# Strassen's scheme for the feed-forward's first product of the last two blocks of tokens

## The chip, the core and the metric

The kernel runs on one core of a Trainium2 chip. The metric is the device time of one execution in microseconds (us): 754.23 is the median of three executions before the change. An execution that is profiled also leaves a trace, and the engines are named as there: PE is the matrix engine (its weight loads are a row of their own, PEld), DVE the vector engine, ACT the scalar engine, POOL the general one, SP the queue that issues the DMAs.

## The reference

Causal attention with a decay, then a feed-forward (MoE) layer, then a second one with a softmax in it:

```
scores = q k^T / sqrt(64) + decay, causal;  x = softmax(scores) v            # 4 batches, 8 heads, 576 positions
h  = x @ w_in                                                                # 2304 x 512 @ 512 x 2048
y  = maximum(0.01*h, h) @ w_out                                              # 2304 x 2048 @ 2048 x 512
h2 = y @ w2_in                                                               # 2304 x 512 @ 512 x 1024
s  = h2 * softmax(h2);  ln = (s - mean(s)) / sqrt(var(s) + 1e-6) * g_ln
out = ln @ w2_out                                                            # 2304 x 1024 @ 1024 x 512
```

All of it is fp32. The kernel keeps that precision by splitting each operand into a high and a low fp16 part, so that one product takes three matmuls (high x high, high x low, low x high).

## The kernel before, in words

**Stages.** The 2304 tokens are nine blocks of 256. Attention fills the blocks (block 6 and 7 last, tiles `x`). The feed-forward goes through them in `ORDER` = 0, 1, 4, 5, 3, 2, 8, 6, 7, each in two halves g of the hidden dimension (18 units `ffn(blk, g)`). A unit has four pieces k: `hidden` (L988) computes 256 hidden columns of a block in one PSUM tile `ps_f` with 24 matmuls of 256 columns, ACT and DVE turn it into the fp16 pair `g`; then 96 matmuls multiply the four `g` by `w_out` (L1036) into `ps_f`, and the result goes to DRAM (`yp_d`). The second layer (`load_y`, `layer2`, `normal`, `layer2_out`) loads a block's y again, makes the sums that Strassen's scheme wants, and computes its first product with seven products in place of eight (`layer2`, L1083): each is six matmuls of 512 columns. Two of the seven go to `p1` and two to `p2`; each of these is one PSUM tile `ph` of 1024 columns, which is two banks, and a product fills one half of it (`bank`, L1089). DVE joins them (`plus` L1103, `full` L1106), `normal` makes softmax and layer norm, a transposing DMA turns the result, and `layer2_out` multiplies by `w2_out` (24 matmuls of 512 columns for 128 tokens).

**Weights.** `whole` (L898) joins a loaded weight chunk, `split` makes the fp16 pair. `split_w2i` (L959) makes the mixed weights of `layer2`. All weights lie in tiles `wz` of 2 KB a partition: 27, eight more when attention's `qa` is done, and 14 (`NWY`, named `wy`) when attention's memory is opened by `phase2` (L1217).

**The order.** A planner written out in the kernel (`Plan.run`, L195) orders everything. Every operation has a priority (smaller goes first), costs from formulas (L378 to L402) and the buffers it reads and writes, which can be a part of a tile: `(Z, 0)` is one part of Z, and parts don't wait for each other in the plan. Whenever a modelled engine is free, the planner takes the ready operation with the smallest priority and emits it at once. So the program's order, over all engines, is the order of the modelled starts. Each engine then works through its own instructions in that order, and semaphores, which the framework below sets from the order in which instructions touch a tile, hold them apart. Unit n of the feed-forward has priority 1000 + 21.76 n, `layer2` of the t-th block `L2P[t]` (1300 and up), its outputs `OUTP[t]`, the second layer's weights 930 to 950, attention 100 to 470.

Of the kernel before, what the change touches and what calls it, by code (L numbers as in the profile page):

```python
# [7 lines left out]
F32 = mybir.dt.float32  # L8
# [16 lines left out]
NG = NC // 2  # L25
# [16 lines left out]
AV = -2.05  # L42
EP = 1307.15
LD = 10.04
# [14 lines left out]
NYO = 2  # L59
NWY = 14  # L60
NY2 = 2
NHL2 = 2
NTR = 3
PWL = 500.0
DMAR = 320.0
YB_ENGS = ("DVE",)
VB_ENGS = ("DVE",)
# [9 lines left out]
US0 = 21.76  # L77
HST = 2.56
TB = 256
# [43 lines left out]
WEIGHT = {"DVE": 7.06}  # L123
WEIGHT2 = {"DVE": 1.06}
HEAT = 0.25
# [252 lines left out]
def dve(n):  # L378
    return 1.042 * n + 70
# [26 lines left out]
def body(tc, kqa, kq, vt, f, wa, w2i, w2o, gln, out):  # L406
# [491 lines left out]
    def whole(src, prio, lead=None):  # L898

        s, k, low = staged(src, prio, lead)  # L900
        z = P.buf("wz")
        P.op(DVE, dve(512), lambda: joined(z.t.bitcast(I32), low, k), prio, w=[z], r=[s, k], lock=True)
        return z
# [117 lines left out]

    def ffn(blk, g, prio):
        eprio = prio - EP
        first, last = blk not in YO, LEFT.setdefault(blk, 2) == 1
        LEFT[blk] -= 1
# [3 lines left out]
        if first:  # L1029
            YO[blk], YPD[blk] = [P.buf("yo") for q in range(2)], []  # L1030
        gs = {k: hidden(k, XB[blk], prio + HST * i, eprio + i) for i, k in enumerate(GRP[g])}
        for q in range(2):
            ps, yo = P.buf("ps_f"), YO[blk][q]
            for d in range(2):

                def pe(d=d, q=q, ps=ps):  # L1036
                    for k in GRP[g]:
                        for i in range(2):
                            y_mms(ps.t[:, TB * d:TB * d + TB], 2 * k + i, 2 * q + d, gs[k], k == GRP[g][0] and i == 0, k == GRP[g][-1] and i == 1)

                P.op(PE, 6 * len(GRP[g]) * mmr(TB), pe, prio + YD + 4 * q + 2 * d, r=list(gs.values()) + [WO[2 * k + i] for k in GRP[g] for i in range(2)],
                     **({"w": [ps]} if d == 0 else {"rw": [ps]}))
# [14 lines left out]
    def load_y(blk, prio):  # L1057
        yw, sy, y = P.buf("yw"), P.buf("sy"), P.buf("y2")
        for q in range(2):
# [14 lines left out]
        sub_f(X(2), A(1, 0), X(1), 256, prio, S_ENGS, w=[(sy, 2)], r=[yw, (sy, 1)])  # L1074
        pieces = [(512 * e, 512, lambda e=e: four(yw.t[:, 0:1024])[:, e::2], (yw, "e%d" % e)) for e in range(2)] + [(1024, 768, lambda: four(sy.t), sy)]
        for at, n, v, k in pieces:
            copy_f(lambda at=at, n=n: four(y.t[:, 0, at:at + n]), v, n, prio, scale=lambda: ev(IY + blk), w=[(y, (0, at))], r=[k, (EX, ("iy", blk))])
        for at, n, v, k in pieces:
            sub_f(lambda at=at, n=n: four(y.t[:, 1, at:at + n]), v, lambda at=at, n=n: four(y.t[:, 0, at:at + n]), n, prio, scale=lambda: ev(IY + blk),
                  w=[(y, (1, at))], rw=[k], r=[(y, (0, at)), (EX, ("iy", blk))])  # L1080
        return y

    def layer2(tb, y, prio, oprios):  # L1083
# [7 lines left out]
        def prod(p, at, n, pr):  # L1091

            def pe():
                for k in range(2):
                    yh, yl = (y.t[:, j, at + 128 * k:at + 128 * k + 128] for j in range(2))
# [5 lines left out]
            P.op(PE, 6 * mmr(512), pe, pr, r=[y, W2I[0, n], W2I[1, n]], w=[p])  # L1101

# [26 lines left out]
    def normal(tt, blk, ps, st, eprio, oprio):  # L1129
# [57 lines left out]
    with tc.manual_schedule():  # L1187
# [44 lines left out]
        P.op(CTL, 1.0, phase2, 0.0, deps=attn_ops)  # L1232
        P.weight = WEIGHT2
# [63 lines left out]
```

## Time and profile before

| | |
|---|---|
| time, median of 3 executions | 754.23 us (752.92 to 755.57) |
| the profiled execution's own time | 756.95 us |
| its span in the trace | 755.2 us, 15580 instructions |
| busy PE, DVE, ACT, POOL | 698.0, 535.7, 502.6, 324.3 us |
| granted clock of PE, mean | 0.997 |

The span runs from the first to the last instruction; the own time has 1.75 us around it. Busy shares are means over stages with different limits, so the stretches count, not the totals. Matmuls are pipelined: a row's duration holds the time in the pipe, and the price of one matmul is the distance between starts.

### The profile page before, as it was taken

The page shows a single profiled execution, that of the slowest core. Times are in us where ns is not written, and L with a number is a line of the kernel's source. Part 1 is how long each engine was busy: PE and PEld are TensorE (multiplying, and loading weights), DVE is VectorE, ACT ScalarE, POOL GpSimd, SP SyncE. Part 2 cuts the span into 40 slices and gives each one's busy share as a digit, 9 for nine tenths or more (in the row PEclk, how much of TensorE's full clock was granted, in tenths as well). Part 3 has the DMA queues.
Part 4 walks back from the last instruction along what each step waited for, and adds up shares of the span by engine and source line. Part 5 has one row for each costly group of instructions (what it writes and reads, how often), then busy time and mean ns, then how long its engine had stood idle before and what let it go on. Part 6 is the DMA issues. An engine that isn't in the chain of part 4 may idle for free.

```text
span 755.2 us, 15580 instructions
## 1 busy us (share of the span) xinstructions
PE 698.0 (92%) x5603; PEld 533.8 (71%) x5603; DVE 535.7 (71%) x1420; ACT 502.6 (67%) x1160; POOL 324.3 (43%) x439
## 2 busy tenths in 40 slices
PE   0558789999999999999999999999999999999997
PEld 0346678788788888888889888688866665444443
DVE  5988789878878887777875964351657558788760
ACT  2698999897878789999895666312635435444551
POOL 4466878894365158646522481000422213132220
PEclk9999999999999999999999999999999999999999
DMA  7989489747548766667875414010023242343343
GB/s 214 312 240 230 110 215 232 129 102 158 140 96 164 143 160 128 132 136 148 180 125 142 144 40 154 1 57 1 30 57 84 70 84 81 87 112 70 85 93 102
DMA packets 163902, 94.18 MB, mean 125 GB/s; under 512 B 144224, under 2 KB 144240, under 8 KB 163824
## 3 DMA queue, kind: packets, MB, share of 16 engines
q1 hardware_dynamic: 163792, 93.17, 52.2%
q8 instruction: 44, 0.72, 0.4%
q14 instruction: 34, 0.28, 0.1%
q10 hardware_dynamic: 32, 0.02, 0.0%
HBM read 47.95 MB, written 10.06 MB: 77 GB/s over the span
## 4 chain that ended last, share of the span: by engine, by line
PE 70%; ACT 9%; DVE 5%; DMA 3%; issue 2%; POOL 1%; SPq 0%; ACTq 0%; POOLq 0%; DVEq 0%
PE ps_f L524 47%; PE ps_g L524 8%; PE ps_s L524 6%; PE ph L524 5%; PE ps_v L524 4%; DMA wst<-wa 2%; ACT ps_s L734 2%; ACT hl L478 1%; DVE hl L489 1%; ACT xr L818 1%; ACT kq L478 1%; DVE VT L489 1%; ACT ps_f L1003 1%; DMA pt<-hl 1%; ACT wz L478 1%
## 5 line engine op out<-in xcount | busy, mean ns | idle before, releaser
L524 PEld LDWEIGHTS <-wz 128*128 128x128 f16 x2700 | 262.5, 99 | 39.5 <-issue 5.5
L524 PE MATMUL ps_f<-g,wz 128*128 128x256 f16 x828 | 104.8, 276 | 0.2 <-DVE g L1004 0.2
L489 DVE SCALAR_TENSOR_TENSOR hl<-ps_s,st,hl 128x512 f16<-128x512 f32 (+4 forms) x160 | 82.0, 538 | 17.6 <-ACT hl L478 16.2
L734 ACT ACTIVATE ps_s<-ps_s,st 128x512 f32<-128x512 f32 (+4 forms) x160 | 78.7, 492 | 9.9 <-DVE st L787 8.7
L524 PE MATMUL ps_f<-dec,wz 128*128 128x256 f16 x684 | 84.5, 273 | 0.0
L478 ACT ACTIVATE hl<-ps_s,st 128x512 f16<-128x512 f32 (+4 forms) x157 | 76.6, 524 | 8.9 <-DVE st L755 3.5
L493 POOL TENSOR_TENSOR kq<-raw,kq 64x576 fp32r<-64x576 f32 x64 | 78.2, 1225 | 8.5 <-ACT kq L478 4.1
L524 PEld LDWEIGHTS <-qa 128*128 128x128 f16 x756 | 72.8, 98 | 10.3 <-issue 2.0
L524 PEld LDWEIGHTS <-tr 128*128 128x128 f16 x432 | 42.2, 98 | 49.9
L524 PE MATMUL ps_v<-pt,VT 128*128 128x128 f16 (+1 forms) x928 | 60.3, 216 | 13.2 <-DVE xr L821 9.1
L524 PEld LDWEIGHTS <-y 128*128 128x128 f16 x378 | 36.6, 98 | 45.6 <-issue 3.7
L787 DVE CUSTOM_DVE_ANT_0 ps_s<-ps_s,mask 128x128 f32<-128x128 f32 (+3 forms) x128 | 62.3, 494 | 7.6 <-PE ps_s L524 6.2
L524 PEld LDWEIGHTS <-VT 128*128 128x128 f16 x928 | 53.1, 101 | 20.3 <-issue 9.2
L524 PE MATMUL ps_f<-x,wz 128*128 128x256 f16 x528 | 66.1, 279 | 0.0
L524 PE MATMUL ps_s<-kq 128*128 128x512 f32 (+5 forms) x256 | 60.8, 366 | 1.6 <-DVE hl L489 1.5
L1004 DVE TENSOR_TENSOR g<-ps_f,g 128x512 f16<-128x512 f32 x40 | 27.5, 686 | 26.3 <-ACT ps_f L1003 25.6
L524 PEld LDWEIGHTS ps_s<-kq 128*128 128x128 f32 (+1 forms) x256 | 40.9, 191 | 7.0 <-issue 1.3
L524 PE MATMUL ps_f<-sd,wz 128*128 128x256 f16 x330 | 45.0, 273 | 0.0
L821 DVE SCALAR_TENSOR_TENSOR xr<-ps_v,xr 64x256 f32<-64x256 f32 (+1 forms) x96 | 33.9, 353 | 15.3 <-ACT xr L818 13.9
L1003 ACT ACTIVATE ps_f<-ps_f 128x512 f32<-128x512 f32 x72 | 42.5, 590 | 0.3
L524 PE MATMUL ps_f<-wst,wz 128*128 128x256 f16 x330 | 42.3, 273 | 0.0
L1004 DVE TENSOR_TENSOR dec<-ps_f,dec 128x512 f16<-128x512 f32 x32 | 22.0, 687 | 26.7 <-ACT ps_f L1003 26.5
(252 smaller groups left out, 1382.3 us busy)
## 6 DMA issues: line engine op xcount, KB each, us to landing
wst<-wa SPq DMA_DIRECT2D x32, 512.0 KB
raw<-kq SPq DMA_DIRECT2D x16, 480.0 KB
VT<-vt SPq DMA_DIRECT2D x16, 320.0 KB
raw<-yp_d SPq DMA_DIRECT2D x18, 256.0 KB
raw<-w2i SPq DMA_DIRECT2D x8, 512.0 KB
raw<-w2o SPq DMA_DIRECT2D x8, 512.0 KB
out<-ot SPq DMA_DIRECT2D x16, 256.0 KB
raw<-kqa SPq DMA_DIRECT2D x12, 256.0 KB
```

Of the source, the lines that this page charges most:

```text
L478: nc.scalar.activation(o, i, CP, scale=1.0 if scale is None else scale)
L489: nc.vector.scalar_tensor_tensor(o, a, scale, b, op0=ALU.mult, op1=ALU.subtract)
L493: (nc.vector if eng == DVE else nc.gpsimd).tensor_tensor(o, a, b, op=op)
L524: nc.tensor.matmul(o, lhsT=l, rhs=r, start=start, stop=stop)
L734: P.op(ACT, act(W, 1, True) + 93, lambda view=view, j=j, k=k: nc.scalar.activation(view(), view(), AF.Exp, bias=sts.t[:, j:j + 1], scale=- ...
L787: P.op(DVE, dve(W) + 130, lambda i=i, j=j, view=view: nc.vector.tensor_tensor_reduce(view(), view(), mask[:, 512 - 128 * i:640], -0.125, 3 ...
L818: P.op(ACT, act(n, 1, True), lambda: nc.scalar.activation(xr.t[a:a + 64, dst0:dst0 + n], ps.t[b:b + 64, c0:c1], CP, scale=PS), prio, w=[(x ...
L821: P.op(DVE, dve(n) + 60, lambda: nc.vector.scalar_tensor_tensor(xr.t[a:a + 64, dst0:dst0 + n], ps.t[a:a + 64, c0:c1], PS, xr.t[a:a + 64, d ...
L1003: P.op(ACT, act(512, 0, True), lambda: nc.scalar.activation(ps.t, ps.t, AF.Prelu, scale=GS, alpha=0.01), eprio, rw=[ps])
L1004: P.op(DVE, dve(512) + 60, lambda: nc.vector.tensor_tensor(g.t[:, 1], ps.t, g.t[:, 0], op=ALU.subtract), eprio, w=[(g, 1)], r=[ps, (g, 0)])
```

## The change

The last two blocks, 6 and 7, go through the feed-forward's first product together, first for g = 1, then for g = 0 (`PU`). For each of the eight pieces k, `hidden2` takes the place of two calls of `hidden`: seven products of six matmuls (256 columns) instead of 48 matmuls. The first two products, P1 and P6, lie in the halves of one `ps_f` tile X, P5 in half of another, Y, and the four results C11, C12, C21, C22 in the quarters of one `ph` tile Z (C11 and C12 in its first bank). ACT copies P1, and seven sums on DVE make the results. `mixed_w` makes the mixed weights of a piece from the fp16 pairs (into a tile `wt`), `mixed_x` the mixed tokens of the two blocks (into four `wz`). Both work from the moment when attention's memory is open. The second layer's weights are joined only after the last of this mixing (`deps=mixed[-1:]`). `wy` has 3 tiles for 14; eight `wt` tiles are new, and as they come free they become `y2a`, `tr` and `hl2`, which the second layer had as tiles of its own. The second product of block 7 gets its own priorities (`PYS`). The softmax of the second layer waits for its own block's scale (`("s", blk)`) and no longer for the scale of `w2_out` (`"u2"`).

```
-EP = 1307.15
+EP = 1514.57
-NWY = 14
-NY2 = 2
-NHL2 = 2
-NTR = 3
+NWY = 3
+T_HEIRS = ("y2a", "tr", "tr", "hl2", "tr", "tr", "hl2")
-YB_ENGS = ("DVE",)
+YB_ENGS = ("DVE", "ACT")
-HST = 2.56
+HST = 2.72
-GS = 2.0 ** -24
+GS = 2.0 ** -20
+PU = (((6, 7), 1), ((6, 7), 0))
+PYS = (17.44, 130.99)
+WTP = (955.0, 965.0)
+XSP = 959.06
+MX = 3
-L2P = (1300.0, 1366.2, 1370.0, 1390.0, 1410.0, 1430.0, 1450.0, 1470.0, 1476.09)
-OUTP = (1340.0, 1370.0, 1398.97, 1420.38, 1440.0, 1496.99, 1472.1, 1500.0, 1520.0)
-LYP = -1744.46
+L2P = (1300.0, 1366.2, 1370.0, 1388.69, 1410.0, 1428.49, 1437.78, 1470.0, 1476.09)
+OUTP = (1340.0, 1370.0, 1398.97, 1420.38, 1440.0, 1496.99, 1472.1, 1514.45, 1520.0)
+LYP = -4034.93
-WEIGHT2 = {"DVE": 1.06}
+WEIGHT2 = {"DVE": 2.51}
+M_ENGS = ("DVE", "POOL")
+MH_ENGS = ("ACT", "DVE", "POOL")
...
     def load_w2i(k, h, prio):
-        z = ZI[j] = whole(w2i[k, h], prio)
+        z = ZI[j] = whole(w2i[k, h], prio, None, mixed[-1:])
     def load_w2o(c, prio):
-        z = ZQ[c] = whole(w2o[c], prio)
+        z = ZQ[c] = whole(w2o[c], prio, None, mixed[-1:])
...
+    def mixed_w(k, prio, after):
+        za, zb, n, t = P.buf("wz"), P.buf("wz"), P.buf("wz"), P.buf("wt")
+        half = lambda z, h: lambda: z.t[:, 256 * h:256 * h + 256]
+        for z, c in ((za, 2 * k), (zb, 2 * k + 1)):
+            sub_f(lambda z=z: z.t, lambda c=c: W(WI[c], 0), lambda c=c: W(WI[c], 1), 512, prio, M_ENGS, op=ALU.add, w=[z], r=[WI[c]], deps=after)
+        sub_f(half(n, 0), half(zb, 1), half(zb, 0), 256, prio, M_ENGS, w=[(n, 0)], r=[zb])
+        sub_f(half(za, 0), half(zb, 0), half(za, 0), 256, prio, M_ENGS, rw=[(za, 0)], r=[zb])
+        sub_f(half(n, 1), half(zb, 1), half(za, 0), 256, prio, M_ENGS, w=[(n, 1)], r=[zb, (za, 0)])
+        sub_f(half(za, 1), half(za, 1), half(n, 1), 256, prio, M_ENGS, rw=[(za, 1)], r=[(n, 1)])
+        for i, z in enumerate((n, za)):
+            d = lambda j, i=i: pair_of(t.t)[:, j, 512 * i:512 * i + 512]
+            copy_f(lambda d=d: d(0), lambda z=z: z.t, 512, prio, engs=MH_ENGS, w=[(t, (0, i))], r=[z])
+            sub_f(lambda d=d: d(1), lambda z=z: z.t, lambda d=d: d(0), 512, prio, M_ENGS, w=[(t, (1, i))], r=[z, (t, (0, i))])
+        WT[k] = t
+    def mixed_x(p, prio, after):
...
+    def hidden2(k, p, prio, eprio):
+        X, Y, Z, u, ga, gb = P.buf("ps_f"), P.buf("ps_f"), P.buf("ph"), P.buf("hr"), P.buf("g"), P.buf("g")
...
+        P1, P6, P5, C11, C12, C21, C22, r1, u2, u3 = (X, 0), (X, 1), (Y, 0), (Z, 0), (Z, 1), (Z, 2), (Z, 3), (u, 0), (u, 1), (u, 2)
+        for i, (o, xt, xb, w, wb) in enumerate((
+                (P1, old(a11), a11, wold(wa_, 0), wa_), (P6, new(x2), x2, wnew(256), t), (C11, old(a12), a12, wold(wa_, 256), wa_),
+                (C22, new(x3), x3, wnew(0), t), (P5, new(x1), x1, wnew(512), t), (C12, new(x4), x4, wold(wb_, 256), wb_), (C21, old(a22), a22, wnew(768), t))):
...
+            P.op(PE, 6 * mmr(TB), pe, prio + 0.2 * i, w=[o] + ([(ga, "slot"), (gb, "slot")] if i == 0 else []), r=[xb, wb])
+        P.op(ACT, act(256, 0, True), lambda: nc.scalar.activation(at(r1)(), at(P1)(), CP), eprio, w=[r1], r=[P1])
+        def plus(o, a, b, **kw):
+            P.op(DVE, dve(256) + 60, lambda: nc.vector.tensor_tensor(at(o)(), at(a)(), at(b)(), op=ALU.add), eprio, **kw)
+        plus(u2, P6, r1, w=[u2], r=[P6, r1])
+        plus(C11, C11, r1, rw=[C11], r=[r1])
+        plus(u3, C22, u2, w=[u3], r=[C22, u2])
+        plus(C22, P5, u3, rw=[C22], r=[P5, u3])
+        plus(u2, P5, u2, rw=[u2], r=[P5])
+        plus(C12, C12, u2, rw=[C12], r=[u2])
+        plus(C21, C21, u3, rw=[C21], r=[u3])
+        for e, g in enumerate((ga, gb)):
...   # as in hidden: two activations on ACT, one subtraction on DVE, for each of the two blocks
-    def ffn(blk, g, prio):
+    def ffn(blks, g, prio):
...
+            both = {k: hidden2(k, blks, prio + 2 * HST * i, eprio + i) for i, k in enumerate(GRP[g])}
+            gs = [{k: x[e] for k, x in both.items()} for e in range(2)]
+        for blk, gk, at in zip(blks, gs, (YD,) if len(blks) == 1 else PYS):
+            ffn_out(blk, g, gk, prio + at, eprio)
...
-            E(), ps.t, AF.Exp, ..., w=[Eb, (st, 1)], r=[ps, (st, 0), (EX, "u2")])
+            E(), ps.t, AF.Exp, ..., w=[Eb, (st, 1)], r=[ps, (st, 0), (EX, ("s", blk))])
...
+            P.tag("wt", tiles(bp, "wt", NG, [128, 1024], F32))
+            P.tag("g", tiles(bp, "g", 4, [128, 2, 512], F16))
+            P.tag("hr", tiles(bp, "hr", 2, [128, 768], F32))
...
+        for blks, g in [((x,), g) for x, g in UN] + [((x,), g) for x in ORDER for g in range(2) if (x, g) not in UN and (x, g) not in paired] + list(PU):
+            ffn(blks, g, 1000.0 + US0 * n)
+            n += len(blks)
```

`mixed_x` has twelve additions or subtractions of 512 columns and four copies, in the manner of `mixed_w`.

## Rows read from the trace of the kernel before

**Rows 1.** Busy time by stretch: us, then PE, PEld, DVE, ACT, POOL (x instructions), clock, DMA.
```profile
412.00:440.00 28.00, 28.00 (x260) 25.16 (x258) 23.64 (x50) 19.77 (x37) 14.63 (x15) 1.00 0.33 115
440.00:479.00 39.00, 39.00 (x359) 34.89 (x357) 18.40 (x31) 20.46 (x44) 13.92 (x14) 1.00 0.23 82
479.00:520.00 41.00, 40.79 (x334) 32.49 (x333) 16.78 (x41) 8.81 (x16) 1.42 (x2) 1.00 0.07 26
520.00:560.00 40.00, 40.00 (x340) 32.99 (x338) 23.94 (x43) 21.54 (x37) 14.40 (x18) 1.00 0.18 41
640.00:700.00 60.00, 59.70 (x279) 27.12 (x277) 48.47 (x115) 28.50 (x41) 14.14 (x27) 1.00 0.38 92
```
**Rows 2.** Chain that ended last, in order of time: start us, us, what.
```profile
442.26 36.70 PE ps_f L524 x336
746.20 5.19 PE ps_g L524 x24
```
**Rows 3.** What PE waited for, 440 to 756: us in total, times, longest.
```profile
PE ph L524 <- DVE sd L1104: 1.4, 2, 1.2
```
**Rows 4.** Timeline of PE, end of a block's seven products: start us, us, engine, operation.
```profile
485.92 0.81 PE L524 MATMUL ph<-sd,y 128*128 128x512 f16 x3
486.94 0.81 PE L524 MATMUL ph<-wst,y 128*128 128x512 f16 x3 [0.21 <-DVE sd L1104]
...
648.34 0.81 PE L524 MATMUL ph<-sd,y 128*128 128x512 f16 x3
649.30 0.81 PE L524 MATMUL ph<-wst,y 128*128 128x512 f16 x3
...
689.36 0.81 PE L524 MATMUL ph<-wz,y 128*128 128x512 f16 x3
...
702.31 0.81 PE L524 MATMUL ph<-sd,y 128*128 128x512 f16 x3
704.29 0.81 PE L524 MATMUL ph<-wst,y 128*128 128x512 f16 x3 [1.17 <-DVE sd L1104]
```
**Rows 5.** Timeline of DVE beside it.
```profile
648.50 0.69 DVE L1108 CUSTOM_DVE_ANT_0 ph<-ph,wst 128x512 f32<-128x512 f32 x1
649.11 0.14 DVE L1108 DVE_READ_ACCUMULATOR2_ANT s<- 128x1 f32 x1
...
690.21 0.70 DVE L1108 CUSTOM_DVE_ANT_0 ph<-ph,wst 128x512 f32<-128x512 f32 x1 [1.54 <-PE ph L524]
...
703.55 0.68 DVE L1104 TENSOR_TENSOR sd<-ph,sd 128x512 f32<-128x512 f32 x1
704.15 2.35 DVE L493 TENSOR_TENSOR hl<-raw,hl 128x1024 f16<-128x1024 f32 x2
```
**Rows 6.** Prices by form, 440 to 755: line engine op tile shapes xcount | busy us, mean ns | idle.
```profile
L1002 ACT ACTIVATE g<-ps_f 128x512 f16<-128x512 f32 x12 | 7.1, 594 | 18.0 <-PE ps_f L524 18.0
L1104 DVE TENSOR_TENSOR sd<-ps_g,wst 128x512 f32<-128x512 f32 x6 | 4.1, 685 | 1.4 <-PE ps_g L524 1.4
L493 DVE TENSOR_TENSOR raw<-raw 128x256 f32<-128x256 f32 x6 | 2.9, 492 | 0.0
L493 DVE TENSOR_TENSOR wy<-x,wy 128x512 f32<-128x512 f32 x1 | 0.7, 678 | 0.0
L489 DVE SCALAR_TENSOR_TENSOR wz<-wy,ex,wz 128x512 f16<-128x512 f32 x3 | 2.2, 744 | 0.6 <-POOL wz L485 0.6
```
**Rows 7.** Operations on tile xr, 380 to 440: ns min/median/max, first and last start us, forms.
```profile
L818 ACT ACTIVATE xr<-ps_v x9: 216/376/382, 382.7 to 410.6; 64x256 f32<-64x256 f32 x5, 64x64 f32<-64x64 f32 x4
L821 DVE SCALAR_TENSOR_TENSOR xr<-ps_v,xr x9: 205/405/428, 383.6 to 411.0; 64x256 f32<-64x256 f32 x5, 64x64 f32<-64x64 f32 x4
L493 POOL TENSOR_TENSOR x<-xr,x x3: 669/671/1029, 384.6 to 411.9; 128x256 f16<-128x256 f32 x3
```
**Rows 8.** Lines L896 and L1178 from 380 on, same columns; then PE's timeline.
```profile
L896 DVE SCALAR_TENSOR_TENSOR sd<-raw,wk x2: 671/682/693, 400.5 to 529.8; 128x512 int32<-128x512 int32 x2
L1178 ACT ACTIVATE ot<-ps_g,ex x8: 668/687/688, 565.7 to 751.5; 128x512 f32<-128x512 f32 x8
...
490.85 0.82 PE L524 MATMUL ps_f<-sd,wz 128*128 128x256 f16 x6
...
635.96 1.46 PE L524 MATMUL ps_f<-wz,tr 128*128 128x512 f16 x6
```

More of the change, by code (lines that the diff above doesn't have):

```diff
@@ L896, in joined, with whole @@
         nc.vector.scalar_tensor_tensor(o, low(), 13, k.t, op0=ALU.logical_shift_right, op1=ALU.bitwise_or)
-    def whole(src, prio, lead=None):
+    def whole(src, prio, lead=None, deps=()):
         s, k, low = staged(src, prio, lead)
         z = P.buf("wz")
-        P.op(DVE, dve(512), lambda: joined(z.t.bitcast(I32), low, k), prio, w=[z], r=[s, k], lock=True)
+        P.op(DVE, dve(512), lambda: joined(z.t.bitcast(I32), low, k), prio, w=[z], r=[s, k], deps=deps, lock=True)
         return z
@@ L1020, in body @@
     YO, LEFT = {}, {}
-    def ffn(blk, g, prio):
-        eprio = prio - EP
+    WT, SX, mixed = {}, {}, []
+    pair_of = lambda t: t.bitcast(F16).rearrange("p (j n) -> p j n", j=2)
+    def mixed_w(k, prio, after):
[12 more added lines that the diff above has]
+        WT[k] = t
@@ new lines, in mixed_x @@
+    def mixed_x(p, prio, after):
+        (a11, a12), (a21, a22) = XB[p[0]], XB[p[1]]
+        z11, z12, z21, n = (P.buf("wz") for _ in range(4))
+        x = lambda a, j: lambda: a.t[:, j]
+        v = lambda z: lambda: z.t
+        for z, a in ((z11, a11), (z21, a21), (z12, a12)):
+            sub_f(v(z), x(a, 0), x(a, 1), 512, prio, M_ENGS, op=ALU.add, w=[z], r=[a], deps=after)
+        sub_f(v(n), v(z11), v(z21), 512, prio, M_ENGS, w=[n], r=[z11, z21])
+        for j in range(2):
+            sub_f(v(z21), v(z21), x(a22, j), 512, prio, M_ENGS, op=ALU.add, rw=[z21], r=[a22])
+        sub_f(v(z11), v(z21), v(z11), 512, prio, M_ENGS, rw=[z11], r=[z21])
+        sub_f(v(z12), v(z12), v(z11), 512, prio, M_ENGS, rw=[z12], r=[z11])
+        out = []
+        for z in (z21, z11, n, z12):
+            t = P.buf("wz")
+            copy_f(lambda t=t: as_g(t.t)[:, 0], v(z), 512, prio, engs=MH_ENGS, w=[(t, 0)], r=[z])
+            sub_f(lambda t=t: as_g(t.t)[:, 1], v(z), lambda t=t: as_g(t.t)[:, 0], 512, prio, M_ENGS, w=[(t, 1)], r=[z, (t, 0)])
+            out.append(t)
+        SX[p] = out
@@ new lines, in ffn @@
+    def ffn(blks, g, prio):
+        eprio = prio - EP
+        if len(blks) == 1:
+            gs = [{k: hidden(k, XB[blks[0]], prio + HST * i, eprio + i) for i, k in enumerate(GRP[g])}]
+        else:
+            both = {k: hidden2(k, blks, prio + 2 * HST * i, eprio + i) for i, k in enumerate(GRP[g])}
+            gs = [{k: x[e] for k, x in both.items()} for e in range(2)]
+        for blk, gk, at in zip(blks, gs, (YD,) if len(blks) == 1 else PYS):
+            ffn_out(blk, g, gk, prio + at, eprio)
@@ L1039, in pe @@
                             y_mms(ps.t[:, TB * d:TB * d + TB], 2 * k + i, 2 * q + d, gs[k], k == GRP[g][0] and i == 0, k == GRP[g][-1] and i == 1)
-                P.op(PE, 6 * len(GRP[g]) * mmr(TB), pe, prio + YD + 4 * q + 2 * d, r=list(gs.values()) + [WO[2 * k + i] for k in GRP[g] for i in range(2)],
+                P.op(PE, 6 * len(GRP[g]) * mmr(TB), pe, prio + 4 * q + 2 * d, r=list(gs.values()) + [WO[2 * k + i] for k in GRP[g] for i in range(2)],
                      **({"w": [ps]} if d == 0 else {"rw": [ps]}))
@@ L1074, in load_y @@
         sub_f(X(2), A(1, 0), X(1), 256, prio, S_ENGS, w=[(sy, 2)], r=[yw, (sy, 1)])
[L1075 to L1079, printed above, removed]
+        pieces = [(ya, 512 * e, 512, lambda e=e: four(yw.t[:, 0:1024])[:, e::2], (yw, "e%d" % e)) for e in range(2)] + [(yb, 0, 768, lambda: four(sy.t), sy)]
+        for y, at, n, v, k in pieces:
+            copy_f(lambda y=y, at=at, n=n: four(y.t[:, 0, at:at + n]), v, n, prio, scale=lambda: ev(IY + blk), w=[(y, (0, at))], r=[k, (EX, ("iy", blk))])
+        for y, at, n, v, k in pieces:
+            sub_f(lambda y=y, at=at, n=n: four(y.t[:, 1, at:at + n]), v, lambda y=y, at=at, n=n: four(y.t[:, 0, at:at + n]), n, prio, scale=lambda: ev(IY + blk),
                   w=[(y, (1, at))], rw=[k], r=[(y, (0, at)), (EX, ("iy", blk))])
-        return y
+        return ya, yb
     def layer2(tb, y, prio, oprios):
@@ L1091, in prod @@
         def prod(p, at, n, pr):
+            yy, at = y[at // 1024], at % 1024
             def pe():
                 for k in range(2):
-                    yh, yl = (y.t[:, j, at + 128 * k:at + 128 * k + 128] for j in range(2))
+                    yh, yl = (yy.t[:, j, at + 128 * k:at + 128 * k + 128] for j in range(2))
                     wh, wl = (W(W2I[k, n], j) for j in range(2))
@@ L1213, in body @@
         nc.sync.dma_start(glt, gln)
-        for n, (blk, g) in enumerate(UN + tuple((blk, g) for blk in ORDER for g in range(2) if (blk, g) not in UN)):
-            ffn(blk, g, 1000.0 + US0 * n)
         def phase2():
```

53 lines of the change are left out of this document (42 added, 11 removed).

## Prediction

> **What bounds the kernel now.** First the busy time by stretch: from 412 us on PE is busy in 28.00 of 28, 39.00 of 39, 40.79 of 41, 40.00 of 40 and 59.70 of 60 us at the full clock, while DVE has 18.40 of 39 in one stretch and 48.47 of 60 in another [rows 1]. So PE is the bound of this half, and the other engines have room. Then the chain of waits, for the price of a matmul: 336 matmuls of 256 columns in 36.70 us are 109.2 ns each, back to back; 24 of 512 columns take 5.19 us, 216 ns each [rows 2]. Then the waits of PE: from 440 us on only 1.4 us are booked, all as "ph waits for DVE" [rows 3]. It follows that a matmul taken out is worth its full 109 ns, that work put on DVE, ACT and POOL is free as long as PE never waits for it, and that the small item in rows 3 deserves a closer look, because the change uses `ph` in a new way.
>
> **What goes.** Eight pieces with 42 matmuls for 48: 48 x 0.1092 = 5.24 us off PE. Nothing comes onto PE: the second product's matmuls, the seven products of the second layer and its outputs stay as they are.
>
> **What stays in place.** `EP` and `HST` move priorities, but no order before 412 us: epilogues stay ahead of attention (-307 to 63 before, lower after; attention 100 to 470), pieces stay between the same neighbours. I cost this part at 0, between -1 and +1 us, since nothing bounds it from a row.
>
> **Mixing.** It can begin when attention's last operation is done, at about 412 us [rows 7]. The first product of unit 14, the first that it feeds, starts at 490.85 in the trace [rows 8]; without the seven products of the second layer that stand just ahead of it (42 x 0.216 = 9.1 us), whose weights now come later, at about 482. So there are 70 us. A piece's weights take four two-input operations of 512 columns (0.678) and four of 256 (0.492) if all run on DVE: 4.7 us; the tokens take twelve of 512: 8.1 us [rows 6]. Ahead of the first product stand three or four pieces and the tokens, 22 to 27 us; all of it is 46 us, less what POOL takes. DVE is busy for 23.64 + some 19 us of these 70 [rows 1], and its share of the second layer's weights leaves. Hidden: 0. If the cover fails, each us that the mixing is late is at worst a us of PE.
>
> **The second layer's weights** are joined behind the mixing, in few free tiles, so later. Before, the last join is at 529.8 us and the first output leaves PE at 565.7 [rows 8]. From 479 us (482 less 24 matmuls of unit 13) PE has 96 matmuls of unit 13's second product and 720 of the last four units: 816 x 0.1092 = 89 us, to about 568, without a single weight of the second layer, and then up to three blocks of seven products (9.1 us each) that need only `w2_in`. On DVE the weights are 16 joins (0.682), 8 subtractions and up to 22 splits (0.744): 33 us [rows 6, 8], beside some 40 us of what was there and 24 us of the new sums, in 120 us from 450 on. Cost 0, at the far end 6 us (a rival below).
>
> **The new epilogue by itself.** Seven sums of 256 columns from PSUM: the row for 256 columns on DVE reads 0.43, the one for 512 reads 0.685 [rows 6, 7]. A piece needs 7 x 0.43 + 2 x 0.687 = 4.4 us of DVE while PE needs 42 x 0.1092 = 4.59, and less in truth, since the next DVE instruction starts 0.08 before the last ends (704.15 against 704.23) [rows 5]. ACT has 0.38 + 4 x 0.594 = 2.8 us [rows 6, 7]. Both keep up; by rate it costs 0.
>
> **The waits inside `ph`.** This is where I expect the cost. In the second layer the last product fills one bank of `p2` while DVE works on the other bank, and the plan has no dependence between them. Yet at 649.30 PE starts 0.05 after DVE ends on the other bank (649.25), 0.31 later than its own pace (648.34 + 0.65); at 704.29 it starts 0.06 after a DVE sum, 1.33 later than its pace [rows 4, 5]. It also goes the other way: at 690.21 DVE has waited 1.54 us for PE, until 0.20 after PE issued the last column of the other bank's product (689.36 + 0.65) [rows 4, 5]. So the semaphores hold a PSUM tile as a whole, in the program's order. Over nine blocks the last product lost 0.37, 0, 0, 0, 0.31, 0.31, 0.05, 1.33 and 0.12 us (four of these pairs in rows 4): 2.5 us, 0.28 a block.
>
> In `hidden2` four products and five sums share one tile Z. Let a piece start at 0 with DVE free. Products of 0.655 us start at 0 (P1), 0.655 (P6), 1.31 (C11), 1.965 (C22), 2.62 (P5), 3.275 (C12), 3.93 (C21). The planner's own formulas emit u2 at 1.53, the sum on C11 at 2.19 and u3 at 2.84, ahead of product C12; the sum on C22 at 3.50, ahead of product C21. On the chip then: C11's sum waits for product C22 (2.62 + 0.20) and ends at 3.25, u3 at 3.60, so product C12 starts at 3.66 for 3.275: 0.38 lost. C22's sum must wait for product C12 (4.31 + 0.20), ends at 4.94, and C21 starts at 5.00 for 4.31: 0.68 lost. That is 1.06 us a piece, 8.5 for eight: the upper end. The lower end is 0: in later pieces of a group ACT and DVE are still at the previous piece's four activations and two subtractions, the sums are emitted later, and a sum that is emitted behind product C21 delays no product. The nearest row is the second layer's 0.28 a block; I take 0.3 a piece, 2.4 us.
>
> The Trainium skill's page "PSUM — Partial Sum Buffer", section "PSUM bank collisions raise a hardware error", has two engines kept apart per bank. By it the two banks of a `ph` tile would be independent, and only C11 against C12 and C22 against C21 would hold each other; the rows at 649, 690 and 704 show waits across the banks instead, set by the program and not by the memory.
>
> **The tail.** From the first output that uses `ps_f` at 635.96 [rows 8] to the end PE is fed from buffers alone. Now block 7's second product has priorities up to 1485, behind the last `layer2` (1476) and ahead of four outputs' times; but the planner takes whatever is ready, so these 2 x 96 matmuls fill holes as they arise. I cost the tail at 0: up to 1.3 us may be won (half of the 2.5 us above, if the order of the second layer falls better), and up to 3 lost (one output of 5.19 us too few as cover, in part).
>
> **Sum.** Own time 756.95 - 5.24 + 2.4 = 754.1, which is 2.72 above the median of the runs as before; so 754.23 - 2.84 = 751.4 us.
>
> **Rivals.** One: the waits don't bite, because the sums are emitted late or banks are independent: 754.23 - 5.24 = 749.0, or 747.7 with 1.3 us won in the tail. For it: five of nine blocks in the second layer lose at most 0.05 [rows 4]. Against: Z has four products for `p2`'s two.
>
> Two, slower: each piece loses the 1.06 us worked out above. The place is the products C12 and C21, the price 8.5 us, so 754.23 - 5.24 + 8.5 = 757.5. It decides from 5.24 / 8 = 0.66 us a piece on. For it: the row at 704 has 1.33 us for one such wait, and DVE has other work in its queue between the sums. Against: later pieces run with their sums behind.
>
> Three: the second layer's weights are late. Each one of the new sums stands ahead of them (priority about -210 against 930), and the tiles free up only as `w_in` is used up. If PE runs out of feed-forward work at 568 and waits 6 us for them, the time is 751.4 + 6 = 757.4 us. Against: the three blocks of spare products, 27 us.
>
> **How the numbers follow.** 0.3% of the time, 2.26 us, is what a measurement can tell from no change. The forecast (1 to 4 us of waits, 750.0 to 753.0) gets 0.44, of which 0.29 lies below 751.97 and 0.15 within the bound. Rival one 0.22, all faster. Rival two (waits of 4 to 9.5 us, 753 to 758.5) 0.22: 0.11 within, 0.11 slower. Rival three 0.12: 0.02 within, 0.10 slower. Together 0.51 faster, 0.28 the same, 0.21 slower. The range goes from 747.5 (rival one with the tail's gain) to 758.5 (rivals two and three with 1 us for the unbounded terms). Faster alone would be 747.5 to 752.
>
> **What would show it.** Right: 5,555 matmul records for 5,603 (48 fewer); in the two groups of four pieces from about 482 on PE idle for some 2 us, its waits booked on `ph` or `ps_f` against DVE sums of 256 columns, at the sixth and seventh product of a piece; no wait of PE for `wt` or the mixed tokens. Rival one shows the same stretch without idle, rival two with over 5 us. Rival three shows one idle stretch of PE near 568 that ends with `w2_in`'s or `w2_out`'s splits. Wrong altogether would be a difference that begins before 412 us, or a hole of PE in the last 60 us.

## The result, and the profile after

The time after is 759.24 us (median of 4; 758.75 to 759.66) against 754.61 us before (median of 4; 752.92 to 755.57): a ratio of 1.0064, 95% interval 1.0043 to 1.0084. So it is slower by 0.6%, where a faster 751.4 us was forecast; the upper end of the range, 758.5, was passed as well. The profiled execution took 759.66 us, its span is 757.9 us.

What the change takes out is gone as worked out, 48 matmuls; the page's line of PE has 5,555 of them:

```profile
PE 694.2 (92%) x5555; PEld 529.4 (70%) x5555; DVE 540.0 (71%) x1443; ACT 538.5 (71%) x1220; POOL 427.6 (56%) x535
```

The busy time by stretch, in the columns of [rows 1]:

```profile
440.00:479.00 39.00, 39.00 (x360) 34.96 (x359) 28.19 (x46) 18.66 (x39) 19.73 (x18) 1.00 0.12 43
479.00:520.00 41.00, 37.41 (x340) 33.00 (x338) 28.52 (x72) 22.84 (x48) 15.72 (x15) 1.00 0.30 103
520.00:560.00 40.00, 37.52 (x286) 27.69 (x285) 27.94 (x59) 25.87 (x47) 21.95 (x24) 1.00 0.19 67
560.00:600.00 40.00, 38.27 (x273) 26.50 (x271) 28.95 (x72) 27.38 (x44) 28.23 (x40) 1.00 0.33 87
600.00:640.00 40.00, 39.88 (x210) 20.49 (x210) 20.45 (x49) 18.87 (x28) 21.63 (x26) 1.00 0.41 107
640.00:700.00 60.00, 59.61 (x278) 27.10 (x277) 43.30 (x107) 43.52 (x65) 46.77 (x63) 1.00 0.49 109
```

PE was busy without a break from 479 to 560 us but for 0.21 us [rows 1]; now it is idle for 3.59 + 2.48 us there, and for 1.73 in the next 40. The six largest of its waits from 440 us on are these (line numbers have moved: L1090 is the seven sums of a piece, L1104 its subtraction, L1199 and L1203 the second layer's sums, L1234 its softmax, L687 a scale):

```profile
PE ph L529 <- DVE hr L1090: 3.2, 4, 1.2
PE ph L529 <- DVE g L1104: 1.4, 1, 1.4
PE ps_g L529 <- DVE ex L687: 1.3, 2, 1.0
PE ph L529 <- DVE ph L1090: 0.8, 1, 0.8
PE ph L529 <- DVE raw L1234: 0.5, 1, 0.5
PE ps_g L529 <- DVE sd L1199: 0.5, 1, 0.5
```

The 1.4 us of [rows 3] have become some 8 in all. A wait of PE costs a little more than is booked, so I measure it by PE's own pace: the distance between two rows' starts, less 109.2 ns for each matmul of 256 columns or 216 ns for 512 [rows 2], where more than 0.15 us is left. By this measure PE loses 6.31 us in the eight pieces, 3.38 in the second layer's first blocks (540 to 640 us) and 1.25 behind 640, 10.94 in all, against 2.51 in the kernel before.

One piece shows how. PE's timeline, a piece's products C22, C12 and C21:

```profile
528.42 0.82 PE L529 MATMUL ph<-wz,wt 128*128 128x256 f16 x6
529.08 0.82 PE L529 MATMUL ph<-wst,wz 128*128 128x256 f16 x6
530.41 0.81 PE L529 MATMUL ph<-x,wt 128*128 128x256 f16 x6 [0.52 <-DVE hr L1090]
```

and DVE's, with the sum u3 on C22 in the second line:

```profile
528.73 0.49 DVE L488 TENSOR_SCALAR wy<-qa,ex 128x512 f16<-128x512 f32 x1
529.93 0.42 DVE L1090 TENSOR_TENSOR hr<-ph,hr 128x256 f32<-128x256 f32 x1 [0.71 <-PE ph L529]
531.26 0.43 DVE L1090 TENSOR_TENSOR ph<-ps_f,hr 128x256 f32<-128x256 f32 x1 [0.91 <-PE ph L529]
```

u3 reads C22, whose product had issued its last column at 528.42 + 0.65 = 529.07. It starts at 529.93, which is 0.20 behind the last column of product C12 (529.08 + 0.65 = 529.73), in the other bank of the tile. Product C21 then starts 0.06 after u3 ends, at 530.41 instead of 529.74: 0.67 us lost. It is the wait of [rows 4, 5], one sum later than the prediction had it: the sum came into the program behind product C12 and in front of C21. C21 lost 1.40, 1.14, 0.67 and 0.93 us in four pieces and C12 0.64 in one, 4.78 us; four pieces lost nothing there.

Not all of this is a wait for the other bank. C21 lies in the bank of C22, so a sum on C22 that stands in front of C21 holds it with any tile; what the shared tile adds here is that the sum itself had to wait for C12. At the largest gap, the 1.40 us ahead of C21 at 497.97, DVE had waited for no product from 493.49 us on. It had other work, and u3, the last line, came late:

```profile
494.87 1.05 DVE L494 SCALAR_TENSOR_TENSOR wt<-raw,ex,wt 128x512 f16<-128x512 f32 x1
495.85 0.34 DVE L1144 SCALAR_TENSOR_TENSOR yo<-ps_f,ex,yo 128x128 f32<-128x128 f32 x1
496.11 0.67 DVE L1104 TENSOR_TENSOR g<-ph,g 128x512 f16<-128x512 f32 x1
...
497.49 0.42 DVE L1090 TENSOR_TENSOR hr<-ph,hr 128x256 f32<-128x256 f32 x1
```

A kind of wait that the prediction did not price stands in the same trace: a piece takes over the tile Z of the piece before the last, whose last reader is a subtraction on DVE. PE's row of such a product C11 (P5 had gone ahead of it):

```profile
509.37 0.83 PE L529 MATMUL ps_f<-wy,wt 128*128 128x256 f16 x6
511.56 0.81 PE L529 MATMUL ph<-wst,wz 128*128 128x256 f16 x6 [1.36 <-DVE g L1104]
```

That is 1.53 us more, and makes 6.31 in all. By the two timelines at most 2.84 us of it (the 0.67 at 530.41, the 0.64 at C12 and this 1.53) come from work in the other bank; the other 3.47 are waits of C21 for a sum in its own bank that came late.

**Where a difference is measured from.** The first matmul of unit 13's third piece is a mark that both programs reach with the same work of PE behind them, at 473.56 us before and here in the kernel after:

```profile
472.33 0.82 PE L529 MATMUL ps_f<-sd,wz 128*128 128x256 f16 x6
```

Five profiles of programs whose order on PE is the same to that point have it at 469.17, 471.00, 472.00, 472.33 and 473.79 us, so a span alone can mislead by some us either way. From the mark to the end of the span it is 281.64 us before and 285.57 after, +3.9 us. The account: -5.24 for the matmuls, +8.43 for PE's gaps (10.94 less 2.51), +0.42 for the stretch behind the last matmul row (752.84 to 757.9 against 750.56 to 755.2) make +3.6; 0.3 is left.

### The profile page after: what moved, and what is told of

Read it like the earlier page. It is cut to its first block, busy times and chain, and to the rows that moved or that the text cites. A ratio compares the mean times of both kernels' runs of the same rounds, so it can differ in the third digit from the quotient of the medians.

```text
span 757.9 us, 15688 instructions
## 1 busy us (share of the span) xinstructions
PE 694.2 (92%) x5555; PEld 529.4 (70%) x5555; DVE 540.0 (71%) x1443; ACT 538.5 (71%) x1220; POOL 427.6 (56%) x535
## 4 chain that ended last, share of the span: by engine, by line
PE 68%; DVE 13%; ACT 12%; issue 4%; DMA 1%; POOL 1%; ACTq 0%; POOLq 0%; DVEq 0%
PE ps_f L529 46%; PE ph L529 6%; PE ps_s L529 6%; PE ps_g L529 5%; PE ps_v L529 4%; ACT ps_s L739 2%; ACT hl L483 2%; DVE hl L494 2%; DVE wz L901 1%; DVE VT L494 1%; DVE ex L669 1%; ACT xr L823 1%; ACT ph L1103 1%; DVE ph L1090 1%; DVE ps_s L792 1%
## 5 line engine op out<-in xcount | busy, mean ns | idle before, releaser
L529 PEld LDWEIGHTS <-wz 128*128 128x128 f16 x2532 | 245.7, 98 | 39.2 <-issue 7.1
L529 PE MATMUL ps_f<-g,wz 128*128 128x256 f16 x948 | 119.1, 276 | 0.2 <-DVE g L1009 0.2
L529 PEld LDWEIGHTS <-wt 128*128 128x128 f16 x720 | 70.1, 98 | 68.7 <-issue 5.6
L494 DVE SCALAR_TENSOR_TENSOR hl<-ps_s,st,hl 128x512 f16<-128x512 f32 (+4 forms) x160 | 81.8, 538 | 18.4 <-ACT hl L483 16.8
L529 PE MATMUL ps_f<-dec,wz 128*128 128x256 f16 x564 | 71.3, 273 | 0.0
L529 PE MATMUL ps_f<-x,wz 128*128 128x256 f16 x396 | 49.7, 276 | 0.0
L498 POOL TENSOR_TENSOR wt<-raw,wt 128x1024 f16<-128x1024 f32 (+1 forms) x22 | 43.2, 1968 | 6.6 <-ACT wt L483 6.1
L823 ACT ACTIVATE xr<-ps_v 64x256 f32<-64x256 f32 (+1 forms) x96 | 31.1, 324 | 15.6 <-PE ps_v L529 10.6
L1228 ACT ACTIVATE raw<-ph,s,ex 128x1024 f32<-128x1024 f32 x18 | 21.6, 1198 | 21.7 <-DVE s L1227 14.2
L529 PE MATMUL ps_s<-qa 66*128 66x128 f32 (+1 forms) x32 | 12.2, 553 | 26.8 <-DMA qa<-sd 17.3
L490 POOL TENSOR_SCALAR kq<-raw 64x960 fp32r<-64x960 f32 x21 | 21.3, 1015 | 27.0 <-PE ps_s L529 22.7
```

Source lines behind the costliest of these rows:

```text
L490: nc.gpsimd.tensor_scalar(o, i, 1.0 if scale is None else scale, 1.0, op0=ALU.mult, op1=ALU.mult)
L494: nc.vector.scalar_tensor_tensor(o, a, scale, b, op0=ALU.mult, op1=ALU.subtract)
L498: (nc.vector if eng == DVE else nc.gpsimd).tensor_tensor(o, a, b, op=op)
L529: nc.tensor.matmul(o, lhsT=l, rhs=r, start=start, stop=stop)
L823: P.op(ACT, act(n, 1, True), lambda: nc.scalar.activation(xr.t[a:a + 64, dst0:dst0 + n], ps.t[b:b + 64, c0:c1], CP, scale=PS), prio, w=[(x ...
L1228: P.op(ACT, act(1024, 2, True), lambda: nc.scalar.activation(E(), ps.t, AF.Exp, bias=st.t[:, 0:1], scale=ev(SY + blk), accum_out=st.t[:, 1 ...
```

## The experiments

Two theories first. **A:** the semaphores hold a PSUM tile as a whole, so a sum in one bank holds products in the other. **C:** DVE comes to the sums late, because of other work in its queue. The expectations of e1 and e2 also name a **B:** the loss comes from the mixing, the late weights and the second layer. Each run has its ratio to the kernel before on the same chip.

| run | median us | ratio, interval | PE's loss in the pieces | its other loss from the mark on | mark to end |
|---|---|---|---|---|---|
| before | 754.61 | 1 | (none) | 2.51 | 281.6 |
| after | 759.24 | 1.0064 (1.0043 to 1.0084) | 6.31 | 4.63 | 285.6 |
| e0_after | 757.56 | 1.0059 (1.0033 to 1.0085) | 6.34 | 3.93 | 284.9 |
| e1_behind | 758.08 | 1.0041 (1.0016 to 1.0066) | 5.04 | 7.05 | 286.8 |
| e8_lyp | 764.80 | 1.0149 (1.0124 to 1.0175) | 4.74 | 14.46 | 293.8 |
| e10_banks | 756.53 | 1.0037 (1.0017 to 1.0057) | 1.97 | 8.05 | 284.5 |
| e9_banks_lyp | 750.94 | 0.9965 (0.9943 to 0.9986) | 0 | 3.79 | 278.4 |
| e13_again | 751.58 | 0.9967 (0.9950 to 0.9984) | 0 | 3.80 | 278.4 |
| e11_mdve | 755.16 | 1.0018 (0.9999 to 1.0036) | 5.71 | 3.32 | 283.2 |
| e12_all | 757.12 | 1.0041 (1.0020 to 1.0063) | 2.59 | 7.96 | 284.8 |

Losses are by PE's own pace, as above, in us. In e1 two of the gaps stand behind a transposing matmul (128x128 fp32); its price is the distance to the next start where nothing waits, 0.15 us behind a matmul of 256 columns and 0.25 behind one of 512. The runs e2, e3 and e5 stand in their own paragraphs.

**The changed kernel again** (e0_after).

> The changed kernel itself once more, as the measure for the three beside it. All theories: ratio to before 1.004 to 1.008 (757.7 to 760.7 us for 754.6), and in its trace again 5 to 7 us lost by PE in the eight pieces between 478 and 550 us, at products C12 and C21 and where a tile Z is taken over.

The loss in the pieces comes back to 0.03 us (6.34 for 6.31): it belongs to the program, not to one execution.

**Sums behind the last product** (e1_behind).

```
-        plus(C11, C11, r1, rw=[C11], r=[r1])
-        plus(u3, C22, u2, w=[u3], r=[C22, u2])
+        plus(C11, C11, r1, rw=[C11], r=[r1], deps=[last])     # last: product C21
+        plus(u3, C22, u2, w=[u3], r=[C22, u2], deps=[last])
```

> The changed kernel, but the sums that touch Z are issued behind the seventh product of their piece, so that no product can wait for a sum of its own piece. Theory A (PE loses its gain to waits inside the tile Z): the waits of PE on ph for the 256-column sums (4 us booked between 490 and 545 us, some 4.8 with the pipe's tails) go, and the time falls from 759.2 to about 754.5; the wait of 1.36 us for a free Z may grow, because the sums end later. Theory B (the loss is the mixing, the late weights and the second layer's stage): 758 to 760, only the place of the waits moves.

The waits at C12 and C21 are gone, so those sums did hold the products. But the piece ends later, and what it holds is handed on later. PE's waits between 478 and 540 us:

```profile
PE ph L529 <- DVE g L1104: 2.3, 2, 1.7
PE ps_f L529 <- DVE yo L1144: 1.0, 1, 1.0
PE ps_g L529 <- DVE va L669: 0.4, 1, 0.4
PE ph L529 <- DVE dec L1104: 0.3, 1, 0.3
```

`g` and `dec` at L1104 are the subtraction that frees a tile Z. In the pieces 5.04 us are lost instead of 6.31, elsewhere 2.4 us more than before this edit. The time, 758.08 us, is what B expected; A's 754.5 did not come. To order the sums late in one whole tile only moves the wait. The `yo` line has another cause; DVE's timeline ahead of it:

```profile
493.26 3.54 DVE L494 SCALAR_TENSOR_TENSOR wt<-raw,ex,wt 128x512 f16<-128x512 f32 x2
496.73 1.11 DVE L1144 SCALAR_TENSOR_TENSOR yo<-ps_f,ex,yo 128x128 f32<-128x128 f32 x4
```

Two splits of the second layer's tokens took 1.8 us each, 0.744 before [rows 6], while POOL had two-input operations from 493.31 to 497.93 without much of a break. That speaks for C as a second part, beside the rows at 494.87 above.

**One-bank tiles** (e10_banks). The priorities within a piece are left; the results lie in two tiles. A second difference comes with it: the tiles `ph` open only when the last piece is done.

```
-        X, Y, Z, ... = P.buf("ps_f"), P.buf("ps_f"), P.buf("ph"), ...
+        X, Y, Z, V, ... = P.buf("ps_f"), P.buf("ps_f"), P.buf("zb"), P.buf("zb"), ...
-        ..., C11, C12, C21, C22, ... = ..., (Z, 0), (Z, 1), (Z, 2), (Z, 3), ...
+        ..., C11, C12, C21, C22, ... = ..., (Z, 0), (Z, 1), (V, 0), (V, 1), ...
-            P.tag("ph", tiles(pp, "ph", 2, [128, 1024], F32))
+            P.tag("zb", tiles(..., "zb", 4, [128, 512], F32))    # "ph" opens in this memory when the last piece is done
```

> The results of a piece lie in two PSUM tiles of one bank each (C11 and C12 in one, C21 and C22 in the other) instead of one tile of two banks; the tiles `ph` of two banks are opened when the last piece is done. The order of products and sums within a piece is that of the changed kernel. Theory A (a PSUM tile is held as a whole by the semaphores, so a sum in one bank holds products in the other): C11's sum now waits for product C11 alone and C22's sum for C22 and P5, both are over before products C12 and C21 are due, and a tile is handed on bank by bank; PE's loss in the eight pieces falls from 6.5 to at most 2.5 us and the time to 754 to 756.5, unless the second layer, which now starts behind the last piece, gives some back. Theory C (DVE comes to the sums late because of other work in its queue, whatever holds them): the waits at C12 and C21 stay, 5 us or more in the pieces, and the time is 758 to 761.

The loss in the pieces falls from 6.31 to 1.97 us, as A expects and C does not. The time follows by 1.0 us only, 756.53 for the changed kernel's 757.56 beside it, because the second layer's first blocks lose 6.9 us, where they lost 3.38. PE's waits from 478 to 700 us:

```profile
PE ph L529 <- DVE raw L1236: 4.6, 2, 3.2
PE zb L529 <- DVE hr L1092: 1.1, 2, 0.8
PE ph L529 <- DVE s L1205: 0.6, 3, 0.3
PE zb L529 <- DVE zb L1092: 0.2, 1, 0.2
```

`raw` at L1236 is the softmax, which reads a whole `ph` and so holds it. Ahead of the longer of its two waits, which ends at 613.74 us, there was no feed-forward work left: its last row starts at 603.2.

What the pieces still lose are waits within a bank. At the largest one C21 waits for u3; u3 stands in DVE's queue behind the sum on C11, and that one had waited for product C12, which lies in C11's own bank:

```profile
495.79 0.43 DVE L1092 TENSOR_TENSOR zb<-zb,hr 128x256 f32<-128x256 f32 x1 [1.14 <-PE zb L529]
496.13 0.41 DVE L1092 TENSOR_TENSOR hr<-zb,hr 128x256 f32<-128x256 f32 x1
```
```profile
496.60 0.82 PE L529 MATMUL zb<-x,wt 128*128 128x256 f16 x6 [0.84 <-DVE hr L1092]
```

The Trainium skill's page "PSUM — Partial Sum Buffer", section "PSUM bank collisions raise a hardware error", wants PSUM guarded by bank. This run agrees: with one tile for each bank no product of a piece waits for a sum in the other bank.

**One-bank tiles and a later preparation** (e9_banks_lyp, and once more as e13_again). In addition to e10's edit:

```
-LYP = -4034.93
+LYP = -100.0
```

> As the run with one-bank tiles, and the preparation of the second layer's tokens (priority -4035 before) now ranks behind the sums of the pieces (about -200). Theory C: what is left of PE's waits on DVE in the pieces goes, 2 us or more below the run beside it if that one kept the waits. Theory A: within 1 us of the run beside it in the pieces, 754 to 757 in all; a preparation that is too late shows as a wait of PE for y2a or y2b after 550 us.

> One-bank tiles and the preparation behind the sums, a second time beside other runs: 749.5 to 752.5 us, 0.995 to 0.998 of before if the first measurement holds, with at most 1 us lost in the pieces.

Now there is no gap in the pieces, and no hole near 613 us. That is more than either theory expected: the pieces lose 1.97 us less than in e10, which is what C had and not A's 1 us, and the rest of PE's losses falls from 8.05 to 3.79 us, which neither had. The stretches of e9:

```profile
479.00:520.00 41.00, 41.00 (x378) 36.69 (x376) 32.22 (x81) 26.34 (x55) 19.43 (x19) 1.00 0.37 124
520.00:560.00 40.00, 39.30 (x290) 28.10 (x288) 29.72 (x63) 27.36 (x54) 24.25 (x30) 1.00 0.25 86
...
600.00:640.00 40.00, 39.92 (x211) 20.32 (x210) 24.92 (x64) 24.89 (x38) 27.99 (x34) 1.00 0.40 94
```

From the mark on it is 3.2 us shorter than before. This version is faster than both kernels, in two runs of twelve executions each. With 3.0 and 2.3 us below the kernel before on its chip it does not reach the 5.24 us of the rival without waits: what is missing is the second layer's 1.3 us of additional loss, 0.3 us at the end of the span and a remainder.

**The preparation alone** (e8_lyp): the `LYP` line on the changed kernel, Z as it was.

> The changed kernel with the second layer's token preparation ranked behind the sums (priority -100 for -4035) and nothing else: the four results stay in one two-bank tile Z. Theory A (the tile is held as a whole): PE still loses 4 us or more in the eight pieces, and the gain of the run that had both edits was not the preparation's; 757 to 761 us. Theory C (other work of DVE in front of the sums): the loss in the pieces falls below 2.5 us and the time to 753 to 755.

The pieces still lose 4.74 us, and the second layer 13 of the other 14.46; among these is 1.19 us in which a product of a piece waits for a `ph` held by the softmax. The time is outside both forecasts. Four versions can be set side by side now: neither edit 6.31 us in the pieces, the preparation alone 4.74, the tiles alone 1.97, both 0. The tiles take 4.3 to 4.7 us off the pieces, the preparation 1.6 to 2.0, so C is a second part and not the main one. PE's waits from 478 to 640 us, and the stretch in which most of the hole lies:

```profile
PE ph L529 <- DVE raw L1234: 6.4, 3, 4.2
PE ph L529 <- DVE hr L1090: 3.2, 5, 1.1
```
```profile
600.00:640.00 40.00, 33.58 (x167) 16.90 (x167) 29.54 (x68) 20.85 (x31) 25.66 (x34) 0.91 0.26 66
```

The same priority is in the fastest version and in one of the slowest. What it does to the time outside the pieces depends on the order that the planner finds for the second layer with it.

**Mixing on DVE alone** (e11_mdve; e12_all is e9 with the same line).

```
-M_ENGS = ("DVE", "POOL")
+M_ENGS = ("DVE",)
```

> As the changed kernel, but all two-input operations of the mixing on DVE, none on POOL. Theory P (POOL's mixing stretches DVE's operations on SBUF, two-input forms of 0.74 us took 1.05 to 1.8 beside it, and that makes the sums late): PE loses 2 us or more less in the pieces, 755 to 757.5 us, and the two-input forms of DVE are back at 0.68 to 0.75 us. Theory A: the waits at C12 and C21 stay (4 us or more of the 6.5), the time is 758 to 761, or above that where DVE, with up to 20 us more work between 440 and 540, comes late with the mixed weights.

> One-bank tiles and the preparation behind the sums, and all two-input operations of the mixing on DVE. Theory P2 (the 2.4 us that the changed kernel gained by that last edit are the mixing's and come on top): 747.5 to 749.5 us. Theory O (that gain was a different order of the second layer, 560 to 640 us, in which that kernel had fewer waits; it does not add up): 750 to 753 us.

e11 is 2.4 us below the changed kernel beside it, but not for the reason it was made for: the pieces still lose 5.71 us (6.34 beside it), where P wanted 2 us less. P's time came out by luck. Of the two splits at L494 (`wt`) one still took 1.75 us, beside two-input operations that POOL has from other places, and one 0.74 without any. By the mark it is 1.7 us shorter, of which 0.6 lies in the pieces and 0.6 in the second layer. On the one-bank tiles it adds nothing: e12 has the hole at 613 us again, 3.33 us, and is slower than e9 and than both its forecasts. So POOL's share of the mixing is not what holds the pieces; the rest of the 2.4 us is within what two orders of the second layer differ by, and no run shows its place.

**Mixing made, but not used** (e2_mixonly): blocks 6 and 7 go through the plain first product, with 48 matmuls more.

```
-            both = {k: hidden2(k, blks, ...) ...}
+            gs = [{k: hidden(k, XB[blks[e]], ...) ...} for e in range(2)]
```

> The changed kernel with all its mixing, its tiles, its priorities and its late weights, but blocks 6 and 7 go through the first product one by one as before (48 matmuls a piece), and the mixed tiles are made and not used. Theory A: PE has 5.24 us more to do and loses the waits inside Z (6 us), so 757.5 to 759; against the kernel before (754.6) what remains is the loss in the second layer's stage, 2 to 4 us. Theory B: the 5.24 us come on top of what there is, 764.

772.72 us, ratio 1.0227 (1.0194 to 1.0259): neither A's 757.5 to 759 nor B's 764. From 479 to 520 us PE is busy without a break (41.00 of 41), beside the mixing; that it is hidden holds. The total says nothing on it, because PE stands for 14.9 us near the end:

```profile
PE ps_g L529 <- DMA wt<-wt: 14.9, 1, 14.9
```

Block 7's second product ended late here, and with it everything that its second layer needs: the product's last row starts at 709.9 us, for 609.9 in the kernel after.

**Block 7's second product early** (e3_y7early): `PYS = (17.44, 39.2)` for `(17.44, 130.99)`.

> The changed kernel with the second product of block 7 at the distance of a unit (21.76) behind that of block 6, and not at the end. The ps_f tiles become ps_g tiles only after the last use of ps_f, so in the changed kernel the second layer runs with one ps_g until 605 us. If this single tile costs (waits of PE on ps_g for DVE, 1.8 us booked between 550 and 601 us), they go and the time falls by 1 to 2 us to 757.5. If those products are needed as filler, the time stays or rises by up to 3 us, with holes of PE at 560 to 640.

768.91 us, ratio 1.0176 (1.0145 to 1.0207): the direction is that of the filler, the size is three times what was expected at most. The pieces wait as in the changed kernel, and 600 to 640 us has holes; the second line is PE's largest wait from 560 to 640:

```profile
600.00:640.00 40.00, 32.19 (x146) 14.92 (x145) 27.70 (x72) 28.19 (x41) 28.22 (x37) 0.87 0.40 90
```
```profile
PE ph L529 <- DVE raw L1234: 6.0, 3, 2.8
```

PE waits for tiles that the softmax holds, as in e10, and the product that could fill the time is used up: its last row starts at 603.4 us, for 609.9 in the kernel after. That its lack makes the holes is argued, not shown; in e8 a hole ends at 622 us although the product lasts to 613.

**The second layer's sum behind its last product, in the kernel before** (e5_l2behind).

```
+        last = prod((p2, 0), a22, 6, prio + 0.6)
-        plus(u2, (p2, 1), u2, rw=[u2], r=[(p2, 1)])
+        plus(u2, (p2, 1), u2, rw=[u2], r=[(p2, 1)], deps=[last])
```

> The kernel before, but in the second layer the sum that reads one half of p2 is issued behind the last product, which fills the other half. If the semaphores hold the whole tile in the order of issue, PE's waits on ph for DVE (1.4 us booked, 2.5 us with all small ones) go, in exchange DVE waits for that product in every block, and the time is 754.6 less 1 to 2.5 us, or the same where the later sums cost as much. If the waits came from something else (weights, y), the last product starts as late as before.

The waits of [rows 3] go, and others of the same size come; all that is booked from 440 us on:

```profile
PE ph L524 <- DVE s L1108: 1.2, 1, 1.2
PE ps_g L524 <- DMA tr<-hl: 0.7, 1, 0.7
```

754.21 us, ratio 0.9989 (0.9966 to 1.0012): no difference that can be measured.

## Why the prediction was wrong

- **What goes, 5.24 us:** right; e9, in which nothing waits in the pieces, shows 3.2 of it from the mark on, loses 1.3 more in waits elsewhere and 0.3 at the end of the span.
- **What stays in place, 0 (±1):** the order on DVE differs from 358.8 us on, where the kernel before has a join of `wz` that the changed one has later, so "no order before 412 us" was wrong. The mark came 1.2 us earlier than before, well inside what it scatters.
- **Mixing, hidden:** right. No wait of PE for `wt` or the mixed tokens is booked; e2 has it too.
- **The waits inside `ph`, 0.3 us a piece:** this step failed. A sum that holds products, and the place, C12 and C21, were right, the size was not. "The nearest row is the second layer's 0.28 a block; I take 0.3": measured are 4.78 us at C12 and C21, 0.60 a piece. The row was one wait in seven products with two tiles; Z has four products and five sums. With the 1.53 us for handing on a tile Z, which the working left out because it followed a single piece alone, it is 0.79 a piece, 6.31 for 2.4. The working also began "with DVE free": in the trace DVE comes late out of other work, and 3.47 of the 6.31 us are waits within one bank, which the whole-tile hold does not explain by itself. (A smaller slip: the blocks with at most 0.05 us that speak for rival one are four by the prediction's own list, not five.)
- **Rival two:** it said that the waits decide from 0.66 us a piece on, and in the pieces they do: 6.31 is more than the 5.24 won. Its 757.5 us lies nearest to the result, partly by luck, with 8.5 us for the pieces and nothing for the second layer. The case against it, "later pieces run with their sums behind", held in two of the four pieces without loss, the third and the fourth; in the first another unit's product stood between, and in the seventh the sum on C11 ended just in time.
- **The second layer's weights, cost 0:** the weights were not late, and no wait ends with them, so rival three is out. But putting nothing for the second layer's start failed as well. Between 540 and 640 us PE loses 3.38 us, and lost nothing there in the kernel before; with the 6.31 us alone the sum would have given 754.23 - 5.24 + 6.31 = 755.3 us. They are waits for the second layer's own sums, softmax and scales (L1199, L1234, L687). This loss moves from version to version by more than the waits in the pieces: 2.6 us in e9, 6.9 in e10, 13 in e8.
- **The tail, 0 (-1.3 to +3):** 1.25 us are lost behind 640 us against 2.14 before, a gain of 0.9; 0.4 goes at the end of the span.

By the predicted own time of 754.1: +3.9 for the pieces, +3.4 for the second layer's start, -1.3 for the gaps of before that are gone (2.51 less 1.25), +0.7 for the end and what is left over, -1.2 ahead of the mark make 759.6; the profiled execution took 759.66.

Open is what makes the second layer's good and bad orders: the runs show where PE waits there and for what, and no run takes the planner's decisions apart.

## What to carry to other kernels

Where a schedule treats parts of a tile as free of each other, ask what the semaphores hold: give each bank that is filled and drained by itself a tile of its own before a loop starts to interleave products and sums in it. Here that took 4.3 us off the loop's waits, and the rest went when the engine that makes the sums had less other work in front of them; look at its queue too. Follow two or three turns of such a loop, not one, because the price of a late sum is also paid when its tile is taken over. And read a saving on the bound engine together with what comes after it: e10 won 4.3 us in the loop, and 1.0 us of time was left of it.

## What the runs showed of the hardware

A two-input operation of 512 columns on DVE took 0.744 us [rows 6], 1.05 us at 494.87 in the kernel after and 1.8 in e1, beside two-input operations on POOL, while a piece's sums of 256 columns, which read PSUM, stayed at 0.41 to 0.43 us in both runs. The Trainium skill's page "SBUF — State Buffer", section "Who interferes with whom", has one port pair that DVE and POOL can only hold in turn, an instruction at a time; these durations agree.

Behind a hole of PE the granted clock fell for some us. In e10 PE was busy for 0.82 us of the 4 before 614, with one gap of 3.33 us that ends at 613.74. The rows behind it, in the columns of [rows 1]:

```profile
614.00:616.00 2.00, 2.00 (x8) 0.80 (x7) 1.96 (x2) 2.00 (x3) 1.91 (x3) 0.70 0.00 0
616.00:618.00 2.00, 2.00 (x6) 0.76 (x5) 0.21 (x1) 1.01 (x3) 1.70 (x5) 0.50 0.00 0
618.00:620.00 2.00, 2.00 (x11) 0.82 (x9) 1.82 (x4) 0.57 (x1) 0.91 (x1) 0.95 0.00 0
```

0.50 is the lower of the clock's two levels, 1.2 GHz for 2.4, and 0.70 and 0.95 are means over both. PE was busy throughout, and the clock was back at the upper level before 620. A hole therefore cost more than its own length: the next four gaps of PE, none with a wait booked, are 1.67 us together. In the stretches of 40 us with the holes of e3 and e8 the mean clock is 0.87 and 0.91, for 1.00 in the same stretch of the kernel after.
